# Opening of an attention and SwiGLU kernel: values of batch 0 in two transfers per group, and two transpose copies exchanged between ScalarE and VectorE

## The chip, the cores and the metric

The kernel runs on one core of one Trainium2 chip. The core has a matrix engine (TensorE, PE in the profile, its weight loads PEld), VectorE (DVE), ScalarE (ACT), GpSimd (POOL) and SyncE (SP), each with its own instruction queue, and 16 DMA engines that they share. The metric is the device time of one execution in microseconds (us). A core's working memory is SBUF; matrix products are written to PSUM, which this kernel uses as eight banks.

## What is computed

Inputs are q, k and v of shape (8 batches, 8 heads, 576 positions, 64 features) in float32, and three weight matrices. The attention is of the linear kind: a softmax of q over features, a softmax of k over positions, and two products, with no 576 by 576 matrix. A gated feed-forward block follows.

```python
q_s = softmax(q, axis=features)          # (b, h, s, d)
k_s = softmax(k, axis=positions)
kv  = einsum('bhsd,bhse->bhde', k_s, v)  # 64 x 64 per head
x   = einsum('bhsd,bhde->bhse', q_s, kv) # then to (4608 tokens, 512)
out = (silu(x @ w_gate) * (x @ w_val)) @ w_out   # 512 -> 1536 -> 512
```

The output has 4608 rows of 512 float32 values. The products run in bfloat16 with float32 sums.

## The kernel before

**Layout.** Eight heads form two groups of four, `G` = 0 and 1. A loaded tile holds one group of one batch: 128 partitions, two heads per partition row, nine slices (T = 9) of 64 features. `BANKS = ((0, 5), (5, 9))` cuts the nine slices in a first piece of five and a second of four, since nine transposed slices don't fit one PSUM bank. All weights and the whole transposed x (`xt`) stay in SBUF.

**Stages.** The opening computes the attention of batch 0 (576 tokens). Then twelve units of the feed-forward (`m_unit`, one for each 128 of the 1536 hidden columns; 16 matmuls each) run over these 576 tokens. The weights arrive meanwhile. Then come batch 1's attention and the first output products, and after that seven chunks of tokens, in which the units of one chunk, the output products of the previous one and the attention of a later batch are mixed. The whole program is in an order written out by hand (`manual_schedule`): each engine takes its instructions in the order of the lines, and waits where one needs another's result.

**The opening's transfers.** SyncE issues the loads of q and k of both groups (L355 to L357). GpSimd issues, on its own queue, the values of both groups, which these transfers turn from float32 into bfloat16 on the way (`v16`, L358 for group 0 in one piece, L361 for group 1 in two pieces), after k of group 0 has landed. Then come the weights: `w_slice` (L96) in six pairs of wg and wv, of 128, 128, 128, 256, 384 and 512 columns, and `wo_slice` (L104) in four slices. These transfers carry eight semaphores in turn, so that from the ninth on each waits on GpSimd until the transfer eight places before it has landed. SyncE's next load, q of batch 1 (L458), waits until the first slice of wo has landed (`after = w_dma[0]`, L454); all other loads of batches 1 and 2 are queued behind it.

**The opening's arithmetic, group by group.** ScalarE takes the exponentials (`exp_of`, L121). VectorE sums each query row and divides by the sum (`norm_sum` L135, reciprocal L140, `norm_mul` L149 giving `qs`). TensorE transposes `qs` in two pieces (`turn_pe`, L164, PSUM tile `tp`), and `turn_out` (L168, copies at L108 on ScalarE and L110 on VectorE) brings each piece to SBUF as `qt`. `key_sum` (L393) forms the key sums on TensorE, with a reciprocal `kvr` on VectorE (L402). `kv_first` (L404) multiplies keys and values: 36 small matmuls for a group, slice after slice, four per slice. `scale_first` (L417) divides the result by the key sums and gives `kn`: one half on ScalarE (L420), the other on ScalarE too (L422, group 0) or on VectorE (L424, group 1). `x_mm` (L195) multiplies `kn` and `qt` for one group and piece into two PSUM banks, and `x_out` (L210) copies the two banks to `xt`, the first on ScalarE and the second on VectorE. `spin` issues matmuls on zeros, whose results are not used.

PSUM banks are handed out in turn, eight in all. The second bank of `x_mm(0, 0, 0)` is the one that held the second piece of group 0's transposes, and the two banks of `x_mm(0, 1, 1)` are those of `x_mm(0, 0, 0)`. A matmul waits until the former content has been copied out.

The lines that set the order around the change, L431 to L443:

```python
turn_out(0, 0, 0, nc.scalar)
exp_of("k", 0, 1)
turn_out(0, 0, 1, nc.scalar)
norm_mul(0, 1, BANKS)
spin(6)
kv_first(0)
key_sum(1)
scale_first(0, nc.scalar)
turn_pe(0, 1, 0)
turn_pe(0, 1, 1)
turn_out(0, 1, 0, nc.vector)
turn_out(0, 1, 1, nc.vector)
xp0 = x_mm(0, 0, 0), x_mm(0, 0, 1)
```

The softmax here doesn't subtract the row's maximum and nothing guards it: scores larger than these inputs give would overflow.

## Time and profile before

| | |
|---|---|
| median of 5 runs | 311.47 us (311.2 to 312.05) |
| profiled execution | 311.76 us |
| its span | 309.9 us |
| matmul busy (PE) | 301.8 us, 97% of the span |
| VectorE, ScalarE, GpSimd busy | 162.0, 146.2, 33.1 us |
| moved by DMA | 45.78 MB, 148 GB/s on average |

The span is the stretch that the profiler recorded; 1.86 us of the profiled execution lie outside it. The profile's timeline gives start, length and engine for each instruction, and in brackets how long the engine sat idle just before and what ended that. The chain of waits is followed back from the last instruction, at each step to what released it. For a DMA, the issue is when an engine's queue handed it out, and the time to landing runs from there until its data were in place. Granted clock of TensorE was 0.999 of full speed over the execution.

### The profile page before, as it was taken

The page shows a single profiled execution, that of the slowest core. Times are in us where ns is not written, and L with a number is a line of the kernel's source. Part 1 is how long each engine was busy: PE and PEld are TensorE (multiplying, and loading weights), DVE is VectorE, ACT ScalarE, POOL GpSimd, SP SyncE. Part 2 cuts the span into 40 slices and gives each one's busy share as a digit, 9 for nine tenths or more (in the row PEclk, how much of TensorE's full clock was granted, in tenths as well). Part 3 has the DMA queues.
Part 4 walks back from the last instruction along what each step waited for, and adds up shares of the span by engine and source line. Part 5 has one row for each costly group of instructions (what it writes and reads, how often), then busy time and mean ns, then how long its engine had stood idle before and what let it go on. Part 6 is the DMA issues. An engine that isn't in the chain of part 4 may idle for free.

```text
span 309.9 us, 5467 instructions
## 1 busy us (share of the span) xinstructions
PE 301.8 (97%) x2182; PEld 149.4 (48%) x2182; DVE 162.0 (52%) x286; ACT 146.2 (47%) x214; POOL 33.1 (11%) x39
## 2 busy tenths in 40 slices
PE   6899999999999999999999999999999999999995
PEld 2577745554444444454444444444444444444443
DVE  3844477945754566365826492639353334433421
ACT  5843478785674375547464737455043113312300
POOL 2960021510200110002000200000000000000000
PEclk9999999999999999999999999999999999999999
DMA  7999999999346815490739352605310302020133
GB/s 271 192 194 207 277 387 391 352 200 392 79 95 185 340 31 116 123 387 19 144 73 345 111 118 61 187 0 107 71 35 0 70 10 57 3 68 8 26 71 103
DMA packets 43018, 45.78 MB, mean 148 GB/s; under 512 B 19568, under 2 KB 28272, under 8 KB 42992
## 3 DMA queue, kind: packets, MB, share of 16 engines
q1 hardware_dynamic: 34096, 39.95, 43.6%
q0 software_dynamic: 8752, 5.31, 12.0%
q8 instruction: 17, 0.28, 0.4%
q10 hardware_dynamic: 144, 0.16, 0.2%
q14 instruction: 9, 0.07, 0.1%
HBM read 37.75 MB, written 9.44 MB: 152 GB/s over the span
## 4 chain that ended last, share of the span: by engine, by line
PE 84%; DMA 10%; DVE 2%; POOL 2%; ACT 1%; issue 0%; SPq 0%
PE o_ps L317 27%; PE g_ps L284 27%; PE u_ps L284 26%; DMA wo<-in_moe_w_out_dram 4%; DMA q<-in_q_dram 2%; DMA wv<-in_moe_w_val_dram 2%; DMA k<-in_k_dram 2%; PE kv L189 2%; PE xp L245 1%; DVE qs L149 1%; DVE rs L135 1%; PE o_ps L338 1%; POOL wv L96 0%; POOL wg L96 0%; POOL v L361 0%; ACT eq L121 0%
## 5 line engine op out<-in xcount | busy, mean ns | idle before, releaser
L291 ACT ACTIVATE sg<-g_ps 128x512 bf16<-128x512 f32 (+2 forms) x120 | 64.7, 554 | 133.9 <-PE g_ps L284 121.9
L293 DVE TENSOR_TENSOR hr<-sg,u_ps 128x512 bf16<-128x512 bf16 (+3 forms) x120 | 72.5, 617 | 86.4 <-PE u_ps L284 80.7
L284 PE MATMUL g_ps<-xt,wg 128*128 128x512 bf16 (+2 forms) x480 | 111.4, 358 | 0.1
L284 PE MATMUL u_ps<-xt,wv 128*128 128x512 bf16 (+2 forms) x480 | 111.3, 358 | 0.0
L317 PE MATMUL o_ps<-wo,hr 128*128 128x512 bf16 x420 | 93.9, 379 | 0.0
L284 PEld LDWEIGHTS <-wv 128*128 128x128 bf16 x480 | 46.7, 98 | 46.9 <-DMA wv<-in_moe_w_val_dram 0.5
L284 PEld LDWEIGHTS <-wg 128*128 128x128 bf16 x480 | 46.3, 98 | 45.5 <-issue 0.6
L317 PEld LDWEIGHTS <-hr 128*128 128x128 bf16 x420 | 40.9, 98 | 48.7
L110 DVE COPY o_sb<-o_ps 128x512 f32<-128x512 f32 x33 | 22.4, 680 | 39.0 <-PE o_ps L317 39.0
L124 POOL CAST vb<-v 128x1152 bf16<-128x1152 f32 x14 | 18.1, 1298 | 135.9 <-DMA v<-in_v_dram 75.4
L135 DVE TENSOR_REDUCE rs<-eq 128x18 f32<-128x1152 bf16 (+2 forms) x18 | 21.7, 1214 | 13.1 <-ACT eq L121 13.1
L149 DVE TENSOR_TENSOR qs<-eq,rr 128x1152 bf16<-128x1152 bf16 (+2 forms) x18 | 22.2, 1244 | 0.1
L121 ACT ACTIVATE eq<-q 128x1152 bf16<-128x1152 f32 (+2 forms) x18 | 18.3, 1052 | 4.6 <-DMA q<-in_q_dram 4.5
L121 ACT ACTIVATE ek<-k 128x1152 bf16<-128x1152 f32 (+2 forms) x17 | 17.9, 1101 | 0.6 <-DMA k<-in_k_dram 0.6
L291 ACT ACT_TABLE_LOAD x12 | 15.4, 1283 | 0.2
L121 ACT ACT_TABLE_LOAD x11 | 14.1, 1283 | 0.2
L259 ACT CAST xt<-xp 128x512 bf16<-128x512 f32 x14 | 7.8, 587 | 4.5 <-PE xp L245 4.5
L260 DVE CAST xt<-xp 128x512 bf16<-128x512 f32 x14 | 9.0, 683 | 0.7 <-PE xp L245 0.7
L388 PE MATMUL idle<-zero 128*128 128x512 bf16 x20 | 6.5, 480 | 2.7 <-DVE rs L135 1.5
L189 PEld LDWEIGHTS <-ek 64*64 64x64 bf16 x504 | 6.3, 107 | 1.7 <-issue 0.4
L189 PE MATMUL kv<-vb,ek 64*64 64x65 bf16 x504 | 6.7, 194 | 0.0
L245 PE MATMUL xp<-qt,kn 64*64 64x512 bf16 (+1 forms) x112 | 6.7, 292 | 0.0
(44 smaller groups left out, 66.1 us busy)
## 6 DMA issues: line engine op xcount, KB each, us to landing
q<-in_q_dram SPq DMA_DIRECT2D x16, 576.0 KB, 6.4
out_dram<-o_sb SPq DMA_DIRECT2D x70, 128.0 KB, 2.3
k<-in_k_dram SPq DMA_DIRECT2D x12, 576.0 KB, 7.4
v<-in_v_dram SPq DMA_DIRECT2D x12, 576.0 KB, 9.6
wo<-in_moe_w_out_dram POOLq DMA_DIRECT2D x4, 384.0 KB, 15.4
k<-in_k_dram SPq DMA_DIRECT2D x4, 320.0 KB, 8.8
k<-in_k_dram SPq DMA_DIRECT2D x4, 256.0 KB, 10.0
v<-in_v_dram SPq DMA_DIRECT2D x2, 320.0 KB, 6.5
```

The source lines that it names most:

```text
L110: eng.tensor_copy(out=out, in_=in_)
L121: nc.scalar.activation(out=e[:, t0:t1], in_=src[:, t0:t1], func=AF.Exp)
L124: return nc.gpsimd.tensor_copy(out=vbs[G][:, :, :, 0:64], in_=raw["v", b, G].rearrange("p h (t d) -> p t h d", d=64),)
L135: i = nc.vector.reduce_sum(out=rs[:, 2 * t0:2 * t1], in_=eq2[:, 2 * t0:2 * t1, :], axis=mybir.AxisListType.X)
L149: last = eng.tensor_mul(qs[:, t0:t1, :].rearrange("p t (h d) -> p (t h) d", d=64), eq2[:, 2 * t0:2 * t1, :], s["rr"][:, 2 * t0:2 * t1].to_ ...
L189: nc.tensor.matmul(out=kv[g][HALF[h], c:c + 65], lhsT=ek[HALF[g], t, h, :], rhs=vbs[G][HALF[g], t, h, :], start=(t == 0), stop=(t == T - 1),)
L245: nc.tensor.matmul(out=o[h][HALF[g], c:c + 64 * (t1 - t0)], lhsT=kn[HALF[h], g, G, :], rhs=qt[G][HALF[h], t0:t1, 64 * g:64 * g + 64], star ...
L260: nc.vector.tensor_copy(out=xt[:, 2 * G + 1, c0:c0 + 512], in_=main[G][1])
L284: nc.tensor.matmul(out=gu[a][i][:, 0:w_], lhsT=(wg, wv)[a][:, kk, ms], rhs=xt[:, kk, c:c + w_], start=(kk == 0), stop=(kk == KT - 1),)
L291: nc.scalar.activation(out=sg[:, 0:w_], in_=g_ps[:, 0:w_], func=AF.Silu)
L293: nc.vector.tensor_mul(hr[:, m, r:r + w1], sg[:, 0:w1], u_ps[:, 0:w1])
L317: nc.tensor.matmul(out=o_ps, lhsT=hr[:, m, r0:r0 + 128], rhs=wo[:, m, :], start=(m == 0), stop=(m == MT - 1),)
```

## The change

Group 0's values are loaded in two transfers, of five and four slices, as group 1's were before; the first of the four waits for k of group 0. `kv_first(0)` is issued as two calls, one per piece, so that its first 20 matmuls wait for the first transfer alone and the other 16 for the second.

The copy of the second transposed piece of group 0 (`turn_out(0, 0, 1)`) moves from ScalarE to VectorE and stands behind `norm_mul(0, 1)` there. The copy of the first transposed piece of group 1 (`turn_out(0, 1, 0)`) moves from VectorE to ScalarE, behind `scale_first(0)`. On VectorE, the copy of `x_mm(0, 0, 0)`'s second bank now stands before VectorE's half of `scale_first(1)`, where it stood behind it.

On each engine the built program has the same number of compute instructions as before, and one DMA more on GpSimd's queue. The order on TensorE is unchanged; the values product of group 0 and that of group 1 each wait for their pieces in turn. Every weight transfer stands one place later on GpSimd's queue, and q of batch 1 waits for the same slice of wo.

```diff
-        d = nc.gpsimd.dma_start(out=v16[0], in_=head_ap(v, 0, 0))
-        tc.add_manual_dep(d.ins, kd[0].ins.name, SYNC, reason="order of loads")
-        for t0, t1 in BANKS:
-            nc.gpsimd.dma_start(out=v16[1][:, :, 64 * t0:64 * t1], in_=head_ap(v, 0, 1, t0, t1))
+        after = kd[0]
+        for G in range(NG):
+            for t0, t1 in BANKS:
+                d = nc.gpsimd.dma_start(
+                    out=v16[G][:, :, 64 * t0:64 * t1], in_=head_ap(v, 0, G, t0, t1)
+                )
+                if after is not None:
+                    tc.add_manual_dep(d.ins, after.ins.name, SYNC, reason="order of loads")
+                    after = None
...
-        turn_out(0, 0, 1, nc.scalar)
         norm_mul(0, 1, BANKS)
+        turn_out(0, 0, 1, nc.vector)
         spin(6)
-        kv_first(0)
+        kv_first(0, *BANKS[0])
+        kv_first(0, *BANKS[1])
         key_sum(1)
         scale_first(0, nc.scalar)
         turn_pe(0, 1, 0)
         turn_pe(0, 1, 1)
-        turn_out(0, 1, 0, nc.vector)
+        turn_out(0, 1, 0, nc.scalar)
         turn_out(0, 1, 1, nc.vector)
         xp0 = x_mm(0, 0, 0), x_mm(0, 0, 1)
         kv_first(1, *BANKS[0])
         kv_first(1, *BANKS[1])
-        x_out(0, 0, 0, xp0[0], (nc.scalar, None))
+        x_out(0, 0, 0, xp0[0])
         scale_first(1, nc.vector)
-        x_out(0, 0, 0, xp0[0], (None, nc.vector))
         x_out(0, 0, 1, xp0[1])
```

## The prediction

> **What bounds the kernel now.** I read the page's shares first, then the chain of waits in order of time, then the opening's timeline, TensorE's waits, and last the DMA queues. TensorE (PE) is busy 301.8 of 309.9 us, so only its few idle places matter. The windows give 14.07 to 37.89 with 23.78 us of matmul in 23.82 us. Behind 50.86 us the weight loads' waits sum to 3.7 us, over nine places the change does not touch. What can move is the start.

> The chain of waits, in order of time, from 0 to 50 us (start, length, what):

> ```profile
> 7.30 1.43 POOL v L361 x2
> ...
> 10.94 6.24 DMA wv<-in_moe_w_val_dram
> ...
> 18.20 13.89 DMA wo<-in_moe_w_out_dram
> 32.09 0.02 issue
> 32.11 7.04 DMA q<-in_q_dram
> 39.15 0.02 issue
> 39.17 1.17 ACT eq L121
> ...
> 45.01 1.37 DVE qs L149
> 46.38 0.05 issue
> 46.42 0.68 PE tp L164 x9
> ```

> It runs through transfers, not through the opening's arithmetic: the values, the weights, the first slice of wo (which lets SyncE load batch 1's queries), then query work up to the transposes at 46.42. PE reaches the wv slice of unit 1 early and waits:

> ```profile
> 16.04 1.14 PE L284 MATMUL g_ps<-xt,wg 128*128 128x320 bf16 x8
> 17.22 0.85 PEld L284 LDWEIGHTS <-wv 128*128 128x128 bf16 x8 [0.35 <-DMA wv<-in_moe_w_val_dram]
> 21.21 0.85 PEld L284 LDWEIGHTS <-wv 128*128 128x128 bf16 x8 [0.20 <-DMA wv<-in_moe_w_val_dram]
> ```

> Half a unit takes 0.98 us (18.22 to 19.20), so unit 1's second half could have begun at 17.02 instead of 17.23: 0.21 us lost there, and 0.08 at 21.21. The opening arrives ahead of its weights. The DMA engines never pause; the software queue (q0) from 9 to 10 us, from 10 to 11, and from 12.2 to 12.6 (packets, MB, share):

> ```profile
> q0 software_dynamic: 179, 0.19, 119.3%
> ...
> q0 software_dynamic: 272, 0.17, 121.4%
> ...
> q0 software_dynamic: 279, 0.07, 177.3%
> ```

> In the first stretch nearly all packets are the whole group 0 values (1152 B in bf16), in the second the first piece of group 1 (640 B), in the third weight rows of 256 B. The issues, with time to landing:

> ```profile
> v<-in_v_dram POOLq DMA_DIRECT2D x1, 288.0 KB, 4.6
> ...
> v<-in_v_dram POOLq DMA_DIRECT2D x1, 160.0 KB, 4.8
> ...
> v<-in_v_dram POOLq DMA_DIRECT2D x1, 128.0 KB, 4.8
> ```

> Issued at 6.44, 7.30 and 8.01, they land at 11.04, 12.10 and 12.81. So the two pieces of group 1 took 1.77 us of the stream.

> **Part 1: group 0's values in two transfers.** GpSimd issued the whole in 0.86 us; two pieces at 0.716 take 1.43, so every weight issue behind them on POOL is 0.57 us later (wg at 9.29 instead of 8.72). Ninth and later transfers wait for the transfer eight places before; the pairing among weights stays the same. The 0.57 is hidden behind the backlog. wg's first slice was issued by 9.48, the values started some 0.8 us after their issue ended (7.30, first packets about 8.1), so it was ready at 10.3. It landed at 8.72 + 4.8 = 13.52, 0.71 behind the last values piece, which is just its own 512 packets (32 per engine at 0.4 us x 16 / 279 = 23 ns: 0.73). The whole values had begun their 256 packets by 10.0 and landed at 11.04, so landing is 1.0 behind the last start, and wg began at 13.52 - 0.73 - 1.0 = 11.8. Cover: 1.5 us; 0.57 fits. Were the cover gone, it costs 0.57.

> The bytes are the same, the packets smaller. Whole: 256 packets, 16 per engine, at 16/179 us = 89 ns: 1.43 us. Halves: 1.77 us by group 1's landings. Difference +0.34. Another row gives less: unit 256 B packets at 23 ns, and the last wg and wv slices (1024 B, landing at 27.6 and 30.2) 2.6 us / 32 = 81 ns; a line through both gives 91 for 1152 and 52 + 42 for 640 and 512, 16 x 3 ns = +0.05. I take +0.30, near the row of the same tensor and shape; the ends are +0.05 and, with cover gone, 0.57 + 0.34 = +0.91. Below nothing it cannot go through packets.

> [...]

> **Part 2: PE's values product in two parts.** The first half lands near 10.6, the second at 11.04 + 0.30 = 11.34. Twenty of 36 matmuls are done by then (36 take 0.41 us, 11.05 to 11.46), 16 remain, 0.18: the end moves from 11.46 to 11.53. key_sum(1) follows 0.07 late. The next transposes wait for the second qs half (12.16) anyway: hidden, nothing.

> **Part 3: the copies exchanged.** ScalarE loses a 0.57 copy before kn (11.57) and gains a 0.67 copy behind it, done near 12.8 against its next work at 12.92: nothing. VectorE gets qt's second half of group 0 at 12.18 (0.42, to 12.60) in place of the 0.49 first half of group 1. The first xp product at 12.55 needs that copy, and one of its banks is the one the copy empties: +0.11 us on PE. Behind the copy stand kvr (0.10), group 1's second half (0.42, to 13.12); kvr is wanted by 13.4.

> **Part 4: x_out before scale_first(1) on VectorE.** xt (0.48) runs 13.12 to 13.60, then kn (0.28) to 13.88 instead of 13.65: +0.23 for the second half of the next xp product. Against it, that product's last bank is free at 13.60 rather than 14.05, where the old order held it. PE's first weight unit, 14.07 before, starts at 14.1 to 14.25. I take +0.13, between gain -0.05 and loss +0.23. It ends in the wait at 17.22: 17.02 + 0.13 is still ahead of 17.23 + 0.30.

> **Sum.** Weights, wo's first slice (32.09), queries (39.15) and the transposes at 46.42 each move by +0.30; the PE delay (0.13) runs beside, within the 0.21 us of wait and the added 0.30. Behind 46.42 PE takes it on to the end: +0.30. The profiled execution took 311.76 us (span 309.9, 1.86 outside), so 312.06; the median of the runs is 0.29 below it, hence 311.77, said as 311.8. A measurement of this kernel can tell about 0.2%, 0.62 us, from no change; the forecast is 0.1%.

> **Rivals.**
> 1. *The stream is bound by POOL's issues.* Where the queue is ready less than 0.57 us ahead, the weights slip by the issue time too: +0.91, 312.4 by the median. For: issue pitch 0.74 and slice time 0.73 are equal in this stretch, so a lost lead is never regained. Against: the 1.5 us cover. It decides slower from 0.62 in all, so 0.3 of packets plus 0.3 of uncovered issue.
> 2. *The late ring.* Same-sized slices landed at 13.52, 14.27, 15.21, then 17.18 (10.94 + 6.24), 17.78, 18.5: one gap of 1.97 in place of 0.75, kept to the end of the stream. One 16 KB instruction packet was on the DMA engines for 0.98 us between 15 and 16 us. If the moved stream meets it on an engine that is ahead, up to 1.0 us comes back: -1.0 + 0.3 = -0.7, 310.8: the other side. It decides once more than 0.9 us of the lag goes. Against: PE's instructions keep number and order, so the packet comes again. Should a second such packet (24 to 25 us, which now costs nothing) fall on the late engine, it is +0.98 + 0.3, 312.75.
> 3. *Nothing at all.* Packets cost as on the line through the weight rows, +0.05 and PE's 0.13 absorbed: 311.5.

> **How the numbers follow.** Forecast (+0.05 to +0.6): 0.45. Rival 3 or a little under: 0.09. Rival 1 and the second packet of rival 2, slower: 0.33. Rival 2's gain: 0.13. So faster 0.13, same 0.54, slower 0.33. The likeliest case's own range is 311.5 to 312.1. Both signs hold weight, so the 8-in-10 range goes from 311.1 (leaving out most of the gain) to 312.5 (taking in +0.91, leaving out +1.28).

> **What would show it.** Right: the group 0 pieces land near 10.6 and 11.35; group 1's at 12.4 and 13.1; wg at 13.8; TensorE waits at unit 1 at about 17.5, longer than 0.35; wo lands at 32.4, q at 39.45, the transposes start at 46.7. Part 4 shows as kn ending near 13.9. Wrong: wo landing by 32.0 or before (the late engine), or a gap in q0's packets from 10 to 13 us with wo past 32.9 (issue bound), or PE's first weight unit past 14.6, when the opening and not the stream sets the loss.

## The result and the profile after

The changed kernel takes 312.64 us (median; 311.64 to 316.01 over 22 executions), the kernel before 311.5 us beside it (311.05 to 312.55, 41 executions). The ratio of the means is 1.0047, with a 95% interval of 1.0034 to 1.006: about 1.5 us slower (1.1 by the medians), against a forecast of 0.3. The median is above the range's 312.5.

One thing has to be known to read these numbers. The 22 executions fall in two groups by TensorE's mean granted clock. Thirteen, at 0.997 to 1.000, took 311.64 to 312.85 us, median 312.26; nine, at 0.989 to 0.995, took 313.76 to 316.01, median 314.0. The first group is 312.26 - 311.5 = 0.76 above the kernel before. The second adds 9/22 x (314.0 - 312.26) = 0.71. The sum is 1.47 us, or 0.47%. So there are two losses to explain, of about equal size.

The profiled execution is the shortest of the 22 (311.64 us, span 309.9, the same as before's), so its span says nothing of the loss; its opening does. The timeline of the changed kernel (start, length, engine, line, operation, and in brackets the idle time ahead of it and what ended it):

```profile
6.38 3.00 POOL L361 DMA_DIRECT2D v<-in_v_dram  x4 [5.07 <-DMA k<-in_k_dram]
...
11.17 0.32 PE L416 MATMUL kv<-v,ek 64*64 64x64 bf16 x16 [0.57 <-DMA v<-in_v_dram]
...
12.62 0.33 PE L416 MATMUL kv<-v,ek 64*64 64x64 bf16 x20
...
13.28 0.32 PE L416 MATMUL kv<-v,ek 64*64 64x64 bf16 x16 [0.33 <-DMA v<-in_v_dram]
...
14.38 0.66 PE L284 MATMUL g_ps<-xt,wg 128*128 128x320 bf16 x4
...
17.22 0.94 PEld L284 LDWEIGHTS <-wv 128*128 128x128 bf16 x8
```

In the kernel before, the same part of TensorE's timeline was:

```profile
12.82 0.46 PE L411 MATMUL kv<-v,ek 64*64 64x64 bf16 x36
...
14.07 0.66 PE L284 MATMUL g_ps<-xt,wg 128*128 128x320 bf16 x4
```

Four values transfers take GpSimd 3.00 us. Group 0's product is done at 11.5, as before. Group 1's product ran through from 12.82 before; it now stops at 13.28 for its second piece. The first weight unit starts at 14.38 instead of 14.07, and the weight load at 17.22 no longer waits for its slice. The two pieces of group 1, issued at 7.95 and 8.66, with KB and time from issue to landing:

```profile
v<-in_v_dram POOLq DMA_DIRECT2D x1, 160.0 KB, 4.6
v<-in_v_dram POOLq DMA_DIRECT2D x1, 128.0 KB, 4.6
```

They land at 12.55 and 13.23, against 12.10 and 12.8 before (a landing that is worked out as issue plus the time shown is good to 0.05 us). The chain of waits has changed its place with that. It ran through weights, wo and queries; it now goes through the second piece of group 1 into PE's arithmetic (start, length, what):

```profile
6.38 2.28 POOL v L361 x3
8.66 4.57 DMA v<-in_v_dram
13.23 0.04 issue
13.28 0.37 PE kv L416 x16
13.65 0.30 ACT kn L425
...
14.00 0.45 PE xp L202 x8
14.44 0.60 PE g_ps L284 x4
...
38.07 6.04 PE o_ps L317 x28
44.11 0.50 PE tp L164 x9
```

In this execution the transposes come at 46.38, as early as before's 46.42: 0.31 us at 14.38 is all taken up by waits that vanish later. A more usual execution shows otherwise.

### The profile page after: what moved, and what is told of

It is laid out like the page before. It is cut to its first block, busy times and chain, and to the rows that moved or that the text cites. A ratio compares the mean times of both kernels' runs of the same rounds, so it can differ in the third digit from the quotient of the medians.

```text
span 309.9 us, 5468 instructions
## 1 busy us (share of the span) xinstructions
PE 301.8 (97%) x2182; PEld 149.7 (48%) x2182; DVE 161.7 (52%) x286; ACT 146.4 (47%) x214; POOL 33.0 (11%) x40
## 3 DMA queue, kind: packets, MB, share of 16 engines
q0 software_dynamic: 9024, 5.31, 12.2%
## 4 chain that ended last, share of the span: by engine, by line
PE 94%; DMA 3%; POOL 1%; ACT 0%; issue 0%; SPq 0%; DVE 0%
PE g_ps L284 30%; PE u_ps L284 30%; PE o_ps L317 29%; PE kv L189 2%; DMA k<-in_k_dram 2%; DMA v<-in_v_dram 1%; PE xp L245 1%; PE o_ps L338 1%; POOL v L361 1%; PE tp L164 0%; ACT xt L259 0%; SPq L77 0%; PE xp L202 0%; PE kv L416 0%; DVE o_sb L342 0%
## 5 line engine op out<-in xcount | busy, mean ns | idle before, releaser
L284 PE MATMUL g_ps<-xt,wg 128*128 128x512 bf16 (+2 forms) x480 | 111.4, 358 | 0.1
L284 PE MATMUL u_ps<-xt,wv 128*128 128x512 bf16 (+2 forms) x480 | 111.3, 358 | 0.0
L284 PEld LDWEIGHTS <-wv 128*128 128x128 bf16 x480 | 47.0, 98 | 46.4
L284 PEld LDWEIGHTS <-wg 128*128 128x128 bf16 x480 | 46.3, 98 | 45.5 <-issue 0.6
L124 POOL CAST vb<-v 128x1152 bf16<-128x1152 f32 x14 | 17.3, 1242 | 137.0 <-DMA v<-in_v_dram 96.8
L135 DVE TENSOR_REDUCE rs<-eq 128x18 f32<-128x1152 bf16 (+2 forms) x18 | 21.7, 1214 | 12.8 <-ACT eq L121 12.8
L149 DVE TENSOR_TENSOR qs<-eq,rr 128x1152 bf16<-128x1152 bf16 (+2 forms) x18 | 21.7, 1217 | 0.1
L121 ACT ACTIVATE eq<-q 128x1152 bf16<-128x1152 f32 (+2 forms) x18 | 18.3, 1052 | 4.5 <-DMA q<-in_q_dram 4.3
L121 ACT ACTIVATE ek<-k 128x1152 bf16<-128x1152 f32 (+2 forms) x17 | 17.9, 1102 | 1.0 <-DMA k<-in_k_dram 0.9
L291 ACT ACT_TABLE_LOAD x12 | 15.4, 1283 | 0.2
L121 ACT ACT_TABLE_LOAD x11 | 14.1, 1283 | 0.2
## 6 DMA issues: line engine op xcount, KB each, us to landing
out_dram<-o_sb SPq DMA_DIRECT2D x70, 128.0 KB, 2.3
```

The lines of the kernel that those rows point to most:

```text
L121: nc.scalar.activation(out=e[:, t0:t1], in_=src[:, t0:t1], func=AF.Exp)
L124: return nc.gpsimd.tensor_copy(out=vbs[G][:, :, :, 0:64], in_=raw["v", b, G].rearrange("p h (t d) -> p t h d", d=64),)
L135: i = nc.vector.reduce_sum(out=rs[:, 2 * t0:2 * t1], in_=eq2[:, 2 * t0:2 * t1, :], axis=mybir.AxisListType.X)
L149: last = eng.tensor_mul(qs[:, t0:t1, :].rearrange("p t (h d) -> p (t h) d", d=64), eq2[:, 2 * t0:2 * t1, :], s["rr"][:, 2 * t0:2 * t1].to_ ...
L284: nc.tensor.matmul(out=gu[a][i][:, 0:w_], lhsT=(wg, wv)[a][:, kk, ms], rhs=xt[:, kk, c:c + w_], start=(kk == 0), stop=(kk == KT - 1),)
L291: nc.scalar.activation(out=sg[:, 0:w_], in_=g_ps[:, 0:w_], func=AF.Silu)
```

## The experiments

They were made in four sets, each on one chip with the kernel before measured beside it; the ratios are to that.

### The change again, and its two halves

**e1_again** is the changed kernel once more, for a trace of a usual execution.

> The changed kernel once more, beside the others on one chip. Of its 22 recorded executions 13 took 311.6 to 312.9 us at a mean granted clock of 0.997 to 1.000, and 9 took 313.8 to 316.0 us at 0.989 to 0.995; none of the 41 of the kernel before took over 312.6. Clock theory: the loss is in TensorE's granted clock in part of the executions, so that the executions again fall into two groups, about 2 us apart, the upper one with a lower clock; a trace that falls into the upper group shows where the clock is low, and it is in the opening (before 20 us). Stream theory: the groups are chance, and all executions are 0.3 to 0.9 us above the kernel before at a clock near 1.00.

It took 312.43 us, ratio 1.0031 (1.0012 to 1.005). Three of 12 executions came at a clock of 0.993 or 0.994 (313.82 to 314.17), and one at full clock took 313.66. Its profiled execution took 312.27 us, span 310.5. TensorE's timeline of it:

```profile
13.23 0.35 PE L416 MATMUL kv<-v,ek 64*64 64x64 bf16 x20 [0.23 <-DMA v<-in_v_dram]
13.97 0.32 PE L416 MATMUL kv<-v,ek 64*64 64x64 bf16 x16 [0.39 <-DMA v<-in_v_dram]
14.69 0.45 PE L202 MATMUL xp<-qt,kn 64*64 64x320 bf16 x8 [0.40 <-ACT kn L425]
15.07 0.66 PE L284 MATMUL g_ps<-xt,wg 128*128 128x320 bf16 x4
```

Both pieces of group 1 are waited for, and land 5.2 us behind their issues (13.20 and 13.91). The first weight unit starts at 15.07, 1.00 us later than before. Of this, the waits for weights in later units give back 0.21 at unit 1, 0.08 at 21.2, 0.05 at 25.1 and 0.1 at 46.4: 1.00 - 0.44 = 0.56, and the transposes start at 46.99 against 46.42, +0.57. The span is 0.6 longer. That is the first loss as this execution had it. But a second way to the same delay runs close beside it: the first slice of wo landed at 32.74 instead of 32.09, and batch 1's first queries at 39.62 instead of 39.15. The work on them began at 39.74, held by ScalarE's work for the last units; by these numbers the queries would have come 0.47 late even with the opening on time.

**e2_split** and **e3_copies** each take one half of the change. The first keeps the loads and the two calls of `kv_first(0)`, with copies as before; the second keeps the copies and the new place of `x_out`, with group 0's values whole.

```diff
 e2_split, on the kernel before: the four loads of the change, and
-        kv_first(0)
+        kv_first(0, *BANKS[0])
+        kv_first(0, *BANKS[1])
 e3_copies, on the kernel before: the turn_out and x_out lines of the change
```

> Only the values of group 0 in two transfers, with the values product issued in two parts; the copies and the order on VectorE as before. Stream theory: it has the whole loss, ratio about 1.001 to 1.005, since group 1's second piece lands 0.4 us later and with it TensorE's first weight unit. Clock theory: it has the upper group of executions if the waits for the value pieces leave TensorE idle for the stretch that matters: ratio 1.003 to 1.006 with a few executions near 314 us at a clock of 0.99. Copies theory: the loss is from the exchanged copies, and this run is within 0.1% of before.

> Only the exchanged copies and the earlier copy of the xp bank on VectorE; group 0's values in one transfer as before. Stream theory and clock theory with the split as its cause: within 0.1% of before, no execution above 312.7 us. Copies theory: ratio 1.003 to 1.006 and executions near 314 us.

e2_split: 312.44 us, ratio 1.0025 (1.0009 to 1.0041), 2 of 12 executions at a clock of 0.994 or 0.995. e3_copies: 311.63 us, ratio 0.9995 (0.9978 to 1.0011), none below 0.997. The loss belongs to the split transfers; a cost of the exchanged copies can't be told from nothing. With them alone, group 1's product runs through again (timeline of e3_copies):

```profile
12.80 0.46 PE L411 MATMUL kv<-v,ek 64*64 64x64 bf16 x36
...
14.08 0.66 PE L284 MATMUL g_ps<-xt,wg 128*128 128x320 bf16 x4
```

In this execution the second half of unit 1 starts at 17.03, without a wait, though the values and weights are loaded as before. So the wait for wv at 17.22, through which the chain before ran, is not in every execution of the same transfers.

The profiled execution of e2_split (313.78 us) is of the second group, and shows what that is. In stretches of it: from and to in us, length, TensorE's busy time and matmuls, its granted clock, DMA share, GB/s:

```profile
11.06:14.47 3.41, 2.19 (x78) 1.00 1.37 148
14.47:17.88 3.41, 3.15 (x19) 0.50 1.71 175
```

TensorE stood still for 0.59 and 0.40 us ahead of group 1's two pieces (13.26 and 14.01), and at 14.47 its clock fell to half, for 3.41 us, with the weight units about to begin. The first unit's second four matmuls start 0.94 us after its first four there (16.30 and 15.36), and 0.50 us after them in e1_again (15.57 and 15.07). By that about half of the 3.41 us is lost, an estimate of 1.7 us, against the 1.74 between the two groups. Half clock for 3.41 us of 310 takes 0.0055 off the mean clock, which is what marks the group. The drop had the same length, 3.41 or 3.42 us, in three profiled executions; it began at 14.47 here, at 14.20 in e5_whole and at 7.31 in e4_spin8. TensorE was not idle ahead of it: it was busy for 2.19 of the 3.41 us before, for 2.05 in e5_whole and for 1.41 in e4_spin8.

### Is it the gap, the number of transfers, or the time of issue?

**e4_spin8** puts two more idle matmuls into the gap ahead of group 0's product (`spin(6)` becomes `spin(8)`).

> The changed kernel with eight instead of six idle matmuls ahead of the values product, so that about 0.43 us more of the waits of TensorE are filled with work. Clock theory: the upper group of executions goes or gets rare, no more than 1 in 10 above 313.5 us, and the ratio falls to 1.000 to 1.003. Stream theory: no change against the changed kernel, or 0.1 us slower.

312.39 us, ratio 1.0032 (1.0008 to 1.0057), with 2 of 12 executions at a low clock and above 313.5 still: not what the clock theory expected. It fills only the first gap; those from 13 to 14 us, ahead of group 1's pieces, are untouched. Its profiled execution had the half clock from 7.31 to 10.72, ahead of the weight units. Its mean clock was 0.995, and it took only 312.32 us: a low mean clock alone does not make an execution long, and where the drop falls seems to matter.

**e5_whole**, on the kernel before, loads group 1 whole too: two values transfers in place of three.

```diff
-        for t0, t1 in BANKS:
-            nc.gpsimd.dma_start(out=v16[1][:, :, 64 * t0:64 * t1], in_=head_ap(v, 0, 1, t0, t1))
+        nc.gpsimd.dma_start(out=v16[1], in_=head_ap(v, 0, 1))
```

> The kernel before with the values of group 1 in one transfer too, so two values transfers in place of three (the change has four). In the split kernels TensorE's first weight unit starts at 14.4 to 15.4 us in place of 14.1, since group 1's pieces land at 13.2 and 13.9 in place of 12.1 and 12.8. Theory of the transfers (more pieces, later group 1): here group 1 lands no later than 12.8 and wg's first slice before 13.5; TensorE starts its units within 0.3 us of 14.1; ratio 0.998 to 1.001. Packet theory alone (small packets of group 1 cost 0.3 us): stream 0.3 us earlier, wo's first slice at 31.8.

311.89 us, ratio 1.0019 (0.9998 to 1.0041): eight executions at 311.22 to 312.04, four at 313.31 to 314.48, two of these at 0.993 and 0.994. The landing by 12.8 did not come: in the profiled execution (313.76 us, clock 0.994) group 1 landed at 13.73, 6.4 us after its issue at 7.33, and PE waited for the whole of it. Fewer issues alone did not bring the data sooner there, and the half clock, from 14.20, came with the gap (1.21 us, up to 13.79). Its issue at 7.33 was no later than that of group 1's first piece before (7.30), so in this execution something other than a later issue made the landing late. The run doesn't tell the theories apart.

**e6_small** keeps the kernel before, group 0 whole, and puts a transfer of 8 KB between the values of the two groups, whose data are not used. It was meant to cost an issue and hardly any stream.

```diff
         d = nc.gpsimd.dma_start(out=v16[0], in_=head_ap(v, 0, 0))
+        nc.gpsimd.dma_start(out=small, in_=...)   # 128 partitions x 2 x 16 of v
```

> The kernel before with one small extra transfer on GpSimd's queue (256 packets of 32 B, 8 KB, into a tile nobody reads) between group 0's whole values and group 1's pieces. Group 1 is issued later by about one issue, 0.6 to 0.9 us, as in the change, while group 0's packets stay large. Issue theory: group 1's pieces land 0.6 to 1.2 us later than before (12.7 to 13.3 and 13.4 to 14.0), TensorE's first unit starts at 14.6 to 15.1, ratio 1.001 to 1.004. Packet theory: they land within 0.2 us of 12.1 and 12.8, ratio within 0.05%.

312.57 us, ratio 1.0035 (1.0019 to 1.0051), 2 of 12 executions at 0.994 and 0.995. Timeline of GpSimd's queue:

```profile
7.27 0.72 POOL L361 DMA_DIRECT2D small<-in_v_dram  x1
7.99 1.43 POOL L368 DMA_DIRECT2D v<-in_v_dram  x2
```

and the issues of group 1's pieces, with time to landing:

```profile
v<-in_v_dram POOLq DMA_DIRECT2D x1, 160.0 KB, 4.5
v<-in_v_dram POOLq DMA_DIRECT2D x1, 128.0 KB, 4.5
```

Issued at 7.99 and 8.70 instead of 7.30 and 8.01, the pieces land at 12.5 and 13.2, nearly as in the changed kernel's profile, but somewhat sooner than the issue theory expected. TensorE's first unit starts only 0.28 us late (14.6 to 15.1 was expected), and the chain of this execution (313.21 us) runs elsewhere. Timeline of TensorE, then the chain:

```profile
14.35 0.67 PE L284 MATMUL g_ps<-xt,wg 128*128 128x320 bf16 x4
```

```profile
18.39 15.09 DMA wo<-in_moe_w_out_dram
33.48 0.02 issue
33.49 7.11 DMA q<-in_q_dram
...
47.83 0.05 issue
47.88 0.68 PE tp L164 x9
```

GpSimd's issues follow one another almost without a pause up to wo, wo lands 1.39 us later than before, and the transposes start 1.46 later: the way of the prediction's rival 1, through weights and queries. One more transfer on GpSimd's queue thus makes a loss of the same size, low clock included, with group 0's packets as large as before. It does not show that the time of issue does it. The 256 added packets of 32 B took 25 ns each by the trace's records, up to 16 x 25 ns = 0.40 us on each of the 16 engines, as much as the 0.4 by which group 1's landings moved. The next run tells the two apart.

### Issue early

**e7_early** is the changed kernel with its first values transfer waiting for the first queries instead of the first keys. The first issue on GpSimd's queue comes at 4.92 instead of 6.38, and those behind it sooner by as much.

```diff
-            load("q", q, 0, G)
-            kd.append(load("k", k, 0, G))
+            kd.append(load("q", q, 0, G))
+            load("k", k, 0, G)
```

> The changed kernel, but its first values transfer waits for q of group 0 in place of k of group 0, so that GpSimd starts to issue about 1.4 us sooner (near 5.0 in place of 6.4). Issue theory: all four pieces land sooner, group 1's by 12.8 at the latest, TensorE's first unit starts by 14.3, and the loss is gone (ratio 0.998 to 1.001), unless q and k of group 1, which share the engines, land so much later that they set the opening. Packet theory: the stream's end does not move, wo's first slice lands at 32.2 to 32.8 as in the changed kernel, ratio 1.002 or more.

311.87 us, ratio 0.9995 (0.998 to 1.0011), no execution of 12 below a clock of 0.997. The pieces land at 12.00 and 12.71, and the loss is gone with all four transfers in place. Group 1's product runs through again:

```profile
12.91 0.46 PE L416 MATMUL kv<-v,ek 64*64 64x64 bf16 x36
...
14.19 0.67 PE L284 MATMUL g_ps<-xt,wg 128*128 128x320 bf16 x4
```

This is the run that decides: the number and size of the packets are those of the changed kernel, and only the issue is earlier. The pieces now spend 5.5 us from issue to landing, so it seems to be the stream that holds them, and the packets show their own price. The software queue from 10.0 to 10.4, 10.4 to 10.8 and 10.8 to 11.2 us (packets, MB, share), in the changed kernel:

```profile
q0 software_dynamic: 69, 0.04, 104.0%
...
q0 software_dynamic: 96, 0.06, 106.2%
...
q0 software_dynamic: 98, 0.06, 119.2%
```

and in e7_early:

```profile
q0 software_dynamic: 136, 0.07, 136.0%
...
q0 software_dynamic: 137, 0.08, 138.7%
...
q0 software_dynamic: 146, 0.08, 138.1%
```

Packets of 640 and 512 B pass at about 350 per us over 16 engines in e7_early, 46 ns each on an engine. A group in two pieces is 2 x 16 x 46 = 1.47 us, the whole was 1.43: by these rates the split costs 0.04 us of stream, where 0.30 had been taken. By landings it is about 0.1: group 1's two pieces came 1.5 us behind group 0 here, and in e3_copies too.

e7_early has two groups of its own, at full clock: five executions at 310.77 to 311.1, seven at 311.73 to 312.32. Its profiled one (312.32) shows what may set them apart:

```profile
41.69 1.14 POOL L124 CAST vb<-v 128x1152 bf16<-128x1152 f32 x1 [20.26 <-DMA v<-in_v_dram]
41.73 2.31 DVE L149 TENSOR_TENSOR qs<-eq,rr 128x1152 bf16<-128x1152 bf16 x1
```

GpSimd's cast of batch 1's values starts just ahead of VectorE's multiply, which takes 2.31 us instead of 1.36; behind it wait the transposes, on the chain.

**e10_early** is the same edit on the kernel before.

> The kernel before with its first values transfer waiting for q of group 0 instead of k of group 0, so that GpSimd issues the values some 1.4 us sooner; nothing else. Lead theory (a values piece whose issue ends less than about 2 us before the queue reaches it is slowed, one with more than 2.5 us isn't): group 1's pieces pass at 350 packets per us instead of 270, landing 0.3 us sooner (11.8 and 12.5), no packet over 0.3 us between 10 and 12 us; ratio 0.996 to 1.000, with executions 1 us apart where the cast of batch 1's values falls together with a VectorE multiply. Packet theory: the pieces still pass at 270 per us.

311.33 us, ratio 0.9989 (0.9975 to 1.0004). Group 1 landed at 12.16 and 12.77, no sooner than before, a miss, though no packet from 10 to 12 us took over 0.3 us, as expected; the first weight unit starts at 13.95. So it was not a late issue that held these pieces in the kernel before. The lead theory's bounds of 2 and 2.5 us were the author's estimate; no run shows them.

**e12_hold** asks the opposite, whether the weight transfers behind delay group 1: the first wg slice is held until group 1's first piece has landed.

> The changed kernel with the first weight transfer held on GpSimd's queue until the first piece of group 1's values has landed. The weights come late by this, some 2 us or more, so only the landing of group 1 is read. If GpSimd's work on the weight transfers slows group 1's pieces, they now land by 12.3 and 13.0 and no packet between 10 and 12 us takes over 0.4 us. If it is their own late issue, they are as late as in the changed kernel: 12.5 to 13.2 and 13.2 to 13.9.

One execution, 315.86 us. Its timeline:

```profile
12.69 0.77 POOL L96 DMA_DIRECT2D wg<-in_moe_w_gate_dram  x1 [3.33 <-DMA v<-in_v_dram]
...
16.10 0.66 PE L284 MATMUL g_ps<-xt,wg 128*128 128x320 bf16 x4 [1.76 <-DMA wg<-in_moe_w_gate_dram]
```

Group 1 landed at 12.40 and 13.11, between what the two theories expected: undecided. The loss is the weights', held too long.

Over all traces, the second piece of group 1, which ends the product, lands at 13.1 to 14.0 in the nine kernels that issue four transfers behind k of group 0. It lands at 12.3 and 12.7 in the two that issue the same four behind q (e11_early_cast below and e7_early), and at 12.5 and 12.8 in e3_copies and the kernel before. There are two exceptions, with group 0 whole: e5_whole (13.7), and e15_before_early_cast below (13.4).

### The clock

**e8_fill** and **e9_fill2** keep the changed kernel's late landings and put idle matmuls into the gaps around group 1's product: three ahead, two between its halves and two behind in e8, two and two in e9.

```diff
+        fill = spin(3)              # e9_fill2: spin(2)
         kv_first(1, *BANKS[0])
+        spin(2, idle=fill)
         kv_first(1, *BANKS[1])
+        spin(2, idle=fill)          # e8_fill alone
```

> The changed kernel with seven idle matmuls (0.22 us each) put where TensorE waits: three ahead of the values product of group 1, two between its halves and two behind it. Clock theory: none of the executions above 313.5 us at a clock under 0.996 is left (the changed kernel and the split alone had 14 in 46), while the lower group stays 0.2 to 0.4% above before, since the late pieces stay: ratio 1.002 to 1.004. If the clock falls for another reason, 3 or 4 in 12 executions are again near 314 us.

> The changed kernel with four idle matmuls where TensorE waits for group 1's values: two ahead of the product's first half, two between the halves, none behind. At 0.22 us each they fit into the waits of the typical execution (0.40 and 0.39 us), so the first weight unit should start near 15.0 to 15.2, as without them. Clock theory: no execution loses a 3.4 us window of half clock at 14 to 18 us, so none is above 313.5 us with a mean clock under 0.996 (the changed kernel: 12 of 34), and the median stays at 312.0 to 312.6, ratio 1.001 to 1.003. If the idle matmuls don't matter, 3 to 5 of 12 are near 314 us again.

e8_fill: 313.03 us, ratio 1.0045 (1.003 to 1.006), 6 executions; e9_fill2: 312.84 us, ratio 1.0042 (1.0025 to 1.006), 12 executions, the median 0.2 above what was expected. No execution fell below a clock of 0.997. But nothing was gained by it: the lower part is later (the first weight unit starts at 15.37 and 15.32), and five executions of e9_fill2 lay at 313.35 to 313.98 at full clock (five more at 313.31 to 313.66 were in e1_again, e2_split, e4_spin8 and e5_whole). The profiled execution of e8_fill (313.33 us) has the same collision as e7_early's:

```profile
42.69 1.14 POOL L124 CAST vb<-v 128x1152 bf16<-128x1152 f32 x1 [20.70 <-DMA v<-in_v_dram]
42.91 2.13 DVE L149 TENSOR_TENSOR qs<-eq,rr 128x1152 bf16<-128x1152 bf16 x1
```

So the collision became a rival for the second loss as well. The slow execution of e2_split speaks against it: there the cast was over at 44.03, and the multiply, begun at 44.13, took its usual 1.36. Two runs test it.

### The collision taken away

In the runs of this section the cast is held until the multiply is done.

```diff
-        norm_mul(1, 0)
+        first_mul = norm_mul(1, 0)
...
-        cast_v(1, 0)
+        c = cast_v(1, 0)
+        tc.add_manual_dep(c.ins, first_mul.ins.name, SYNC, reason="order of the vector port")
```

**e13_cast** does so in the changed kernel, **e14_fill2_cast** in e9_fill2.

> The changed kernel, with GpSimd's first cast of batch 1 held until VectorE's first multiply of batch 1's queries is done. Two causes are proposed for the executions of the changed kernel near 314 us. Clock theory: TensorE's half-rate stretch costs them 1.7 us, whatever VectorE does; about three in ten executions still come at 313.5 to 314.2 us with a mean clock of 0.993 to 0.995, and the others stay at 311.8 to 312.9 us, median 312.3 to 312.6. Port theory: the multiply that takes 2.1 to 2.3 us in place of 1.36 beside the cast makes them; then none is above 313 us, whatever the clock. Executions at full clock between 313 and 314 us, of which the kernels with the later values had one in twelve and the filled one five in twelve, are laid to the multiply by both; none should be left.

> The two pairs of idle matmuls around group 1's values product and the held cast together. Clock and port are then both taken away: no execution at a mean clock below 0.996, none above 313.1 us, median 312.4 to 312.8 (the lower group of the filled kernel was 312.45 to 312.96). If executions at 313.4 to 314 us remain as in the filled kernel without the held cast, the multiply did not make them and their cause is open.

e13_cast: 312.82 us, ratio 1.004 (1.0026 to 1.0054). Three of 12 executions still come at 313.62 to 313.94, at a clock of 0.993 to 0.995; the other nine at 312.32 to 313.18, median 312.51, 1.0 above the 311.51 of before. The collision does not make the second loss; the clock does. Two executions at full clock, 313.15 and 313.18, are a little above what was expected. e14_fill2_cast: 312.98 us (312.62 to 314.1, 7 executions), ratio 1.0046 (1.003 to 1.0062), none below 0.997. The group at 313.4 of e9_fill2, measured on another chip, is gone but for one execution, 314.1 at a clock of 1.0; what made that one is open.

Over all runs: with four transfers issued late and the gaps around group 1 unfilled (the changed kernel, e1_again, e2_split, e4_spin8, e13_cast) 19 of 70 executions lay above 313.5 us at a low clock; with e6_small it is 21 of 82. With the gaps around group 1 filled it was 0 of 25, which at 21 in 82 each would have a chance of (61/82) to the 25th, 0.0006, if executions are independent. The evidence of the same chips alone is thinner: 0 of 13 filled (e8_fill, e14_fill2_cast) against 5 of 24 (e6_small, e13_cast). With an early issue (e7, e10, e11, e15) it was 0 of 46, in the kernel before 1 of 158.

**e11_early_cast** is e7_early with the held cast.

> The changed kernel with the early issue of the values, and with GpSimd's cast of batch 1's first values made to wait for VectorE's multiply of group 0 of batch 1. With the early issue alone 5 of 12 executions took 310.8 to 311.1 us and 7 took 311.7 to 312.3; in the recorded one of the latter that multiply took 2.31 us instead of 1.36 while the cast ran. Port theory: the second group goes, all executions 310.6 to 311.4, ratio 0.997 to 0.999. If the two groups have another cause, both are still there.

311.19 us (311.0 to 311.67, 11 executions), ratio 0.9983 (0.9968 to 0.9997): some 0.4 us below the kernel before, with an interval that ends barely under 1. e7_early's upper group is gone, though e7 ran on another chip, where no version with the held cast was measured. Timeline:

```profile
41.81 1.36 DVE L149 TENSOR_TENSOR qs<-eq,rr 128x1152 bf16<-128x1152 bf16 x1
43.24 1.14 POOL L124 CAST vb<-v 128x1152 bf16<-128x1152 f32 x1 [22.22 <-DVE qs L149]
```

**e15_before_early_cast** asks whether that gain needs the change at all: early issue and held cast on the kernel before.

> The kernel before with its first values transfer waiting for the first queries in place of the first keys, and with the held cast: the change's two transfers per group and its exchanged copies are left away from the version that beat both kernels. If early issue and the held cast carry the whole gain: 311.0 to 311.3 us, ratio 0.998 to 0.999, and no execution above 312. If the split group 0 still adds something once the issue is early: 311.4 to 311.6.

311.49 us (311.01 to 312.15), ratio 0.999 (0.9977 to 1.0004). The median lies with the second theory, that the split group 0 adds something once its issue is early, but the intervals of e11 and e15 overlap, and the two were run on different chips. It is not settled. In the profiled execution (311.98 us) group 0, whole, was issued at 4.86 and landed only at 11.94, 7.1 us later (6.0 in e10_early). Group 1 followed at 12.7 and 13.4, and the first weight unit came late:

```profile
14.74 0.66 PE L284 MATMUL g_ps<-xt,wg 128*128 128x320 bf16 x4
```

So an early issue does not always mean an early landing.

## Why the prediction was wrong, step by step

**What bounds the kernel.** The chain through weights, wo and queries was read rightly for the execution that was profiled (e3_copies, with the same transfers, does not have its wait for wv), and so was the slack that the opening had: the waits of the weight units took up 0.44 us of its delay in e1_again. "The opening arrives ahead of its weights" held only as long as the opening's delay stayed below that.

**Part 1, the step that failed.** It said that the 0.57 us of later issue were "hidden behind the backlog" under a cover of 1.5 us, which was worked out for the first weight slice and taken to cover group 1's values too. For group 1 the later issue was thus put at nothing without a reason, and that is the step that failed. With four transfers issued behind k of group 0 its second piece landed at 13.1 to 14.0 in all nine traces, instead of 12.8; with the same four issued 1.46 us sooner it landed at 12.7 and 12.3, and e7_early lost nothing. What did not come out is how a later issue makes a later landing: in e1_again 0.70 us of issue became 1.1 of landing, and in the changed kernel half as many packets passed from 10.0 to 10.4 us as in e7_early (69 against 136), some of them long (11 took over 0.3 us from 10 to 12 us). A reading under the cover was wrong too: the last packet of the whole values began at 10.57 by the trace's records, not by 10.0, so the landing at 11.04 was some 0.5 behind it and not 1.0. The shift was mis-sized a little as well: the first transfer costs GpSimd 0.86 us even as a half, so group 1 is issued 0.65 to 0.70 later, not 0.57. The landings expected at 12.4 and 13.1 came at 12.55 and 13.23 in the shortest execution and at 13.20 and 13.91 in a usual one.

**The packet term** of +0.30 was mis-sized: 0.04 by e7_early's rates and about 0.1 by landings, nearer the lower bound of +0.05. The row it was taken from, group 1's 1.77 us, differs between executions: it is 1.5 in e3_copies, with the same transfers.

**The stream.** wo's first slice lands at 32.15 in the shortest execution and at 32.74 in e1_again, against 32.09 before and the expected 32.4. The late ring of rival 2 did shift: unit 1's wv slice landed at 16.4 instead of 17.18, but at 16.7 in e3_copies too, so this is not the split's doing. The lag was back by wo, and brought nothing.

**Part 2** held in its place: group 0's halves land at 10.18 and 11.14, and the product ends at 11.5 (11.53 expected). **Parts 3 and 4** cost less than they were given: e3_copies is at 0.9995, and VectorE's half of kn ended at 13.66 there, not near 13.9. The +0.13 for PE's first weight unit, 14.1 to 14.25, was for the copies only, and with the copies alone it starts at 14.08. In the changed kernel it starts at 15.07, and the sign named for being wrong, "PE's first weight unit past 14.6, when the opening and not the stream sets the loss", is what appeared.

**The rivals.** Rival 1 had the size (+0.91, 312.4; the executions at full clock have their median at 312.26) and half the mechanism, an issue lead that is lost. Its place was the stream of weights. In the changed kernel's traces what comes late first is group 1's values, and the loss travels through PE's opening; but in e1_again the weights and queries were late by nearly as much, and in e6_small the loss went their way. How much each way has in the first loss over all executions is open. Slower by over 0.2% had a chance of 0.33.

**What was not in the prediction at all** is the clock, +0.71 of the 1.47 us. That gaps of 0.59 and 0.40 us on TensorE were followed by a stretch that cost 1.7 more through its clock (e2_split) had no place in any case. The profile before, at a clock of 0.999, gave no sign of it.

## What to carry to other kernels

A cover has to be worked out for each transfer that is moved, the first one behind the new issue above all. Where TensorE begins its main work out of a string of small products, a wait there can be paid twice, as here: once as itself (0.76 us by the medians) and once as a stretch at half clock (0.71 us on the mean, from 9 of 22 executions). The times of many executions beside their mean clocks showed that; the one profile of the changed kernel did not. And before a transfer is cut in two, ask whether its issue can come earlier instead: here 1.5 us of earlier issue undid the loss.
